# Two PSUM banks shared by three users, V of the first batch loaded by block, and matmuls on zeros between the real ones: a chunked attention with an MLP behind it

## The chip, the cores and the metric

The kernel runs on one core of one Trainium2 chip. A core has a matrix engine (TensorE, PE in the profile; its weight loads are a row of their own, PEld), a vector engine (VectorE, DVE), a scalar engine for activation functions (ScalarE, ACT), a general engine (GpSimd, POOL) and an engine that only issues transfers here (SyncE, SP). Every engine works through its own queue in order; semaphores hold an instruction back until what it needs is there. The metric is the device time of one execution in microseconds, as the median of the runs. Matrix products are written to PSUM, eight banks of 2 KB per partition; everything else lives in SBUF or in HBM.

## What is computed

There are 4 batches of 8 heads, 768 positions and head size 64. Each head's queries are taken in chunks of 32. A chunk sees 8 memory keys, its own 32 positions, 16 positions to the left and 8 to the right. The result goes, head by head side by side, through a two-layer MLP with 512 inputs, 2048 hidden columns and 512 outputs.

```python
for c in range(nc):                       # chunks of 32 positions
    l_start = max(0, c_start - left_ctx)  # 16 to the left
    r_end = min(S, c_end + right_ctx)     # 8 to the right
    k_full = np.concatenate([mem_k, k_ctx], axis=2)
    v_full = np.concatenate([mem_v, v_ctx], axis=2)
    scores = scale * np.matmul(q_c, k_full.transpose(0, 1, 3, 2))
    a = softmax(scores)
    out[:, :, c_start:c_end] = np.matmul(a, v_full)
...
h = x @ w_in
s = np.sin(alpha * h)
g = h + s * s / (alpha + 1e-09)
return g @ w_out
```

All inputs and the output are float32; the kernel multiplies in bfloat16 and accumulates in float32.

## The kernel before

The work is ordered by hand: each engine runs its instructions in the order in which the program writes them, and the framework only adds semaphores and picks slots for tiles. A pool with `bufs=n` has n slots per tag; a new tile waits until a slot's last user is done.

**Blocks.** Attention works on 8 blocks (NJ) of 96 queries (three chunks). For a block, `qk_exp` (L244) multiplies the block's keys (104 columns with the 8 memory keys among them, from `kTi`) with its queries (`qT`) for all 8 heads into a score tile `sc`, and takes the exponential in three activations, one for each chunk, with a mask column of `biasm` as the bias. `pv` (L268) multiplies the result `pt` with the block of V (`vw`, with a column of ones for the sum) into `ot`; VectorE takes the reciprocal of the sums (L278) and scales (L279) into `x_blk`. `xt` (L286) transposes `x_blk` on TensorE into `xtp`, and VectorE copies it into `xT` (L292). `burst` (L294) runs these over the blocks, with a product `lag` steps behind its scores and the transpose one step behind the product.

**Preparing q and k.** They arrive as rows; `pair_up` (L206, VectorE) puts two heads side by side, `t_k` and `t_q` (L221, L236) transpose on TensorE, and ScalarE and VectorE copy the result into `kTi` and `qT`. A k or q pair of one head pair is a "piece"; there are 8 to a batch. `put_memk` (L146, VectorE) writes the memory keys of a batch into `kTi`; `put_memv` (L140) the memory values into `vw`.

**MLP.** `l1` (L311) makes one of 16 blocks (`ft`) of 128 hidden columns for all 768 positions: 8 matmuls into `hT` (two banks), the sine on ScalarE into `u` (L322), its square on ScalarE (L327) or, where `dve_sq` says so, on VectorE (L325), and then `gT = s / alpha + hT` on VectorE (L328). `l2` (L334) is a generator: 6 output tiles `o` of 128 positions, each 16 matmuls over `ft`, copied out by VectorE (L351) or ScalarE (L353) and stored by SyncE (L354). It is not run at once: `Stream.take(n)` draws n matmuls from it at places in later work, so that layer 2 of batch i is spread over the attention and the layer 1 of batch i+1.

**Order.** For each batch i: layer 1 (16 blocks, with 2 layer-2 matmuls drawn per block, 3 in the last batch; for i = 1, 2 the pieces of the next batch are put in at fixed blocks, `at_ft`); for i = 0 the 8 pieces come after the blocks; then `put_memk(i + 1)` (L410), the loads of k and q for batch i+2, `burst(i + 1)`, and the loads of V for batch i+2. The first batch's pieces and its `burst` stand ahead of the loop (L358 to L378).

**PSUM.** `big` has three slots of two banks for `sc`, `ot`, `hT` and two of three transpose tiles of the pieces at the start; `opp` has one bank for `o`; `atp` has one bank for `xtp` and the other transpose tiles (`t_tile`, L215).

**Loads.** k, q, V and the weights are converted to bfloat16 on the way, by DMAs that POOL issues one after the other (`dma_start` on `nc.gpsimd`): k and q of batch 0 as 8 pairs (L101), four DMAs for all of V (`load_v_all`, L122), eight of w_in, k and q of batch 1, four of w_out, V of batch 1. Between them POOL makes the mask `biasm` (L169 to L183, 13 selects).

Of the kernel before, what the change touches and what calls it, by code (L numbers as in the profile page):

```python
# [9 lines left out]
P = 128  # L10
QW = 96
NEG = -30000.0
# [33 lines left out]
def kernel(  # L46
# [30 lines left out]
    big = ctx.enter_context(tc.tile_pool(name="big", bufs=3, space=bass.MemoryType.PSUM))  # L77
    opp = ctx.enter_context(tc.tile_pool(name="opp", bufs=1, space=bass.MemoryType.PSUM))
    atp = ctx.enter_context(tc.tile_pool(name="atp", bufs=1, space=bass.MemoryType.PSUM))

# [32 lines left out]
    def load_qk(b):  # L113
# [6 lines left out]
        return kb, qb  # L120

    def load_v_all(b):  # L122

# [22 lines left out]
    def put_memk(b):  # L146
# [3 lines left out]
        )  # L150


    for vw in vws:
# [8 lines left out]
    for b in range(B):  # L162
        nc.sync.dma_start(memk_f[NM * b:NM * b + NM], mem_k[b].rearrange("h n d -> n h d"))
    nc.sync.dma_start(memv_f[64:72].rearrange("n b h d -> n (b h) d"),
                      mem_v.rearrange("b h n d -> n (b h) d"))
    nc.scalar.copy(memk_bf[:], memk_f[:])
    nc.scalar.copy(memv_st[64:72], memv_f[64:72])
    load_v_all(0)
    nc.gpsimd.memset(biasm[:], NEG)  # L169
    steps = (  # L170
        (0, ((0, 0.0), (56, NEG), (64, 0.0), (72, NEG))),
        (1, ((32, 0.0), (96, NEG))),
        (2, ((64, 0.0),)),
        (3, ((16, 0.0), (56, NEG), (64, 0.0), (72, NEG))),
        (4, ((64, 0.0), (120, NEG))),
    )
    for col, seq in steps:
        for thr, val in seq:
            nc.gpsimd.affine_select(
                out=biasm[:, col:col + 1], in_=biasm[:, col:col + 1],  # L180
                compare_op=ALU.is_gt, fill=val, base=thr,
                pattern=[[0, 1]], channel_multiplier=-1,
            )  # L183
    with nc.allow_non_contiguous_dma(reason="alpha transpose load"):
# [4 lines left out]
    for pt in pts:  # L189
        nc.vector.memset(pt[:, H * QW:H * QW + 32], 0.0)  # L190
    nc.vector.reciprocal(inv_alpha[:], alpha_sb[:])

# [22 lines left out]
    def t_tile():  # L215
        state["t"] += 1
        if state["t"] % state["pools"] == 0:
            return atp.tile([P, 6, P], BF, name="tt_a", tag="at")
        return big.tile([P, 6, P], BF, name="tt_b", tag="big")
# [24 lines left out]
    def qk_exp(j):  # L244
# [10 lines left out]
        for m in range(3):  # L255
            col = m
            if j == 0 and m == 0:
                col = 3
            if j == NJ - 1 and m == 2:
                col = 4  # L260
            nc.scalar.activation(  # L261
                pt[:, 0:H * QW].rearrange("p (g e c) -> p e g c", g=4, e=2)[:, :, :, 32 * m:32 * m + 32],
                sc[:, :, 0:4 * QW].rearrange("p g (e c) -> p g e c", e=4)[:, :, :, 32 * m:32 * m + 32],
                ACTF.Exp, bias=biasm[:, col:col + 1], scale=0.125,
            )
# [20 lines left out]
    def xt(xT, j, x_blk):  # L286
        xtp = atp.tile([P, KT, QW], BF, name="xtp", tag="at")
        for kt in range(KT):
# [5 lines left out]
    def burst(b, stream, shares, lag):  # L294
# [3 lines left out]
        for s in range(NJ + lag + 1):  # L298
            n = shares[s] if s < len(shares) else 0
            if s < NJ:  # L300
                ptl[s] = qk_exp(s)
            stream.take(n // 2)
            if 0 <= s - lag < NJ:
# [30 lines left out]
    def l2(i, gT, last=False):  # L334
        for s in range(NSUB):
            if last and s % 3 == 1:
                o = atp.tile([P, d_model], F32, name="o_a", tag="at")
            elif last and s % 3 == 2:
                o = big.tile([P, d_model], F32, name="o_b", tag="big")
            else:  # L340
                o = opp.tile([P, d_model], F32, name="o", tag="o")
            for ft in range(FT):
# [16 lines left out]
    for n in range(2 * HP):  # L359
        (t_k if n % 2 == 0 else t_q)(prs[n], n // 2)  # L360
        if n + 2 < 2 * HP:
            prs.append(pair_up(kq[n % 2], (n + 2) // 2))
    mt = atp.tile([P, HP, 32], BF, name="mt", tag="at")
    for hp in range(HP):
# [3 lines left out]
    put_memv(0)  # L368
    put_memv(1)
    for c in range(8):  # L370
        load_w_in(c)
# [5 lines left out]
    stream = Stream()  # L377
    xT = burst(0, stream, (), 3)  # L378

    for i in range(B):  # L380
# [6 lines left out]
        state["pools"] = 1  # L387

        def piece(n):
            while len(pieces) < min(n + 3, 2 * HP):  # L390
                pieces.append(pair_up(*srcs[len(pieces)]))
            (t_k if n % 2 == 0 else t_q)(pieces[n], n // 2)

        for ft in range(FT):
            dve_sq = (ft % 2 == 1) if i == 0 else (ft % 4 == 3)
            if 0 < i < B - 1:
                if ft == 0:
                    pieces += [pair_up(*srcs[n]) for n in range(2)]
                if ft in at_ft:
                    piece(at_ft[ft])  # L400
            l1(i, ft, xT, gT, dve_sq)
            if 1 <= ft:
                stream.take(3 if last else 2)
        stream.add(l2(i, gT, last))
        if not last:
            if i == 0:
                state["pools"] = 3
                for n in range(2 * HP):
                    piece(n)
            put_memk(i + 1)  # L410
            if i + 2 < B:
                kq_next = load_qk(i + 2)
            if i == 0:
                xT = burst(i + 1, stream, (4,) * 12, 4)
            else:
                xT = burst(i + 1, stream, (5, 6, 7, 7, 7, 7, 7, 7, 7, 7), 1)
            stream.take(3)
            if i + 2 < B:
# [33 lines left out]
```

## Time and profile before

| what | value |
|---|---|
| runs | 279.32, 276.13, 277.3 us; median 277.3 |
| profiled execution | 276.12 us, span 274.4 us, mean granted clock of TensorE 0.98 |
| TensorE busy | 220.0 us, 80% of the span |
| ScalarE busy | 169.8 us, 62% |
| VectorE busy | 150.6 us, 55% |
| moved by the DMA queues | 21.12 MB, mean 77 GB/s |

In rows of the timeline the first number is the start in us from the beginning of the span, the second the time from the first start to the last end of the merged instructions, then engine, line, operation, output <- inputs, sizes and how many. What stands in brackets is how long the engine was idle before, and what ended that idle time. The row PEclk of the page gives the clock granted to TensorE in tenths, in 40 slices of 6.86 us.

### The profile page before, as it was taken

What the parts mean: (1) busy time and instruction counts of PE and PEld (TensorE: products, weight loads), DVE (VectorE), ACT (ScalarE), POOL (GpSimd) and SP (SyncE); (2) the same over time, 40 slices, a digit from 0 to 9 for tenths busy, and PEclk for the clock granted to TensorE, in tenths of its full rate; (3) what the DMA queues carried; (4) which work ended last, traced back from release to release, by engine and by line L of the source; (5) the groups of instructions that cost most, each with busy time, mean ns of one, the idle gap of its engine ahead of it and who ended that gap; (6) DMA issues with size and microseconds to landing.
All of it is one profiled execution on the core that took longest, in us unless ns stands there. A gap on an engine that the chain in (4) does not pass through costs nothing.

```text
span 274.4 us, 4340 instructions
## 1 busy us (share of the span) xinstructions
PE 220.0 (80%) x1706; PEld 126.6 (46%) x1732; DVE 150.6 (55%) x284; ACT 169.8 (62%) x258; POOL 41.4 (15%) x62
## 2 busy tenths in 40 slices
PE   0463988884799799984998898984999889798994
PEld 0352744442545456552454455652455445454441
DVE  2352828898427867675254667776155365576000
ACT  2666727874996199986536199896546178575000
POOL 8984551000530000170000000000000000000000
PEclk9999999999799999999799999999799999999999
DMA  7999999990399900299921101001011110101222
GB/s 79 181 118 129 197 205 206 183 87 3 45 198 156 93 0 0 52 170 147 88 76 41 38 0 41 0 0 41 38 42 38 41 38 0 38 4 38 76 76 76
DMA packets 53740, 21.12 MB, mean 77 GB/s; under 512 B 36312, under 2 KB 50648, under 8 KB 53720
## 3 DMA queue, kind: packets, MB, share of 16 engines
q0 software_dynamic: 47648, 14.42, 73.9%
q1 hardware_dynamic: 6072, 6.43, 7.5%
q8 instruction: 13, 0.21, 0.3%
q14 instruction: 7, 0.06, 0.1%
HBM read 28.95 MB, written 6.29 MB: 128 GB/s over the span
## 4 chain that ended last, share of the span: by engine, by line
PE 53%; ACT 13%; DVE 11%; DMA 11%; POOL 5%; issue 5%; DVEq 0%; POOLq 0%; ACTq 0%
PE o L343 22%; PE hT L315 18%; DMA w_out_sb<-in_moe_w_out_dram 6%; ACT u L322 5%; DMA w_in_sb<-in_moe_w_in_dram 5%; DVE gT L328 4%; ACT s L327 3%; PE o_a L343 3%; PE o_b L343 2%; DVE s L325 2%; DVE o_sb L351 2%; ACT o_sb L353 2%; PE sc L248 2%; PE ot L274 2%; ACT pt L261 1%
## 5 line engine op out<-in xcount | busy, mean ns | idle before, releaser
L315 PE MATMUL hT<-xT,w_in_sb 128*128 128x384 bf16 x512 | 94.4, 332 | 2.7 <-DVE gT L328 1.7
L343 PE MATMUL o<-w_out_sb,gT 128*128 128x512 bf16 x296 | 84.3, 387 | 12.8 <-DVE o_sb L351 5.8
L328 DVE SCALAR_TENSOR_TENSOR gT<-s,inv_alpha,hT 128x768 bf16<-128x768 f32 x64 | 64.9, 1014 | 40.3 <-ACT s L327 37.5
L322 ACT ACTIVATE u<-hT,alpha_sb 128x768 f32<-128x768 f32 x64 | 57.5, 898 | 43.3 <-PE hT L315 43.3
L315 PEld LDWEIGHTS <-w_in_sb 128*128 128x128 bf16 x512 | 50.1, 99 | 39.4 <-issue 6.7
L343 PEld LDWEIGHTS <-gT 128*128 128x128 bf16 x384 | 34.4, 98 | 43.1 <-issue 13.5
L261 ACT ACTIVATE pt<-sc,biasm 128x256 bf16<-128x256 f32 x96 | 37.7, 484 | 24.6 <-PE sc L248 24.5
L327 ACT ACTIVATE s<-u 128x768 f32<-128x768 f32 x44 | 37.1, 843 | 1.4
L278 DVE RECIPROCAL rinv<-ot 96x8 f32<-96x8 f32 x32 | 6.5, 203 | 30.5 <-PE ot L274 30.0
L279 DVE TENSOR_TENSOR x_blk<-ot,rinv 96x512 bf16<-96x512 f32 x32 | 22.0, 687 | 1.1
L325 DVE TENSOR_TENSOR s<-u 128x768 f32<-128x768 f32 x20 | 19.1, 956 | 3.4 <-ACT u L322 3.3
L248 PE MATMUL sc<-qT,kTi 64*128 64x96 bf16 x256 | 12.4, 229 | 8.6 <-DVE kTi L147 7.9
L274 PE MATMUL ot<-vw,pt 128*128 128x65 bf16 x256 | 15.0, 207 | 4.7 <-DMA vw<-in_v_dram 3.9
L274 PEld LDWEIGHTS <-pt 128*128 128x128 bf16 x256 | 13.3, 107 | 11.2 <-issue 4.7
L224 PEld LDWEIGHTS <-pr 128*128 128x128 bf16 x96 | 7.5, 114 | 19.6 <-DVE pr L208 18.2
L292 DVE COPY xT<-xtp 128x384 bf16<-128x384 bf16 x32 | 11.2, 350 | 7.6 <-PE xtp L289 6.7
L248 PEld LDWEIGHTS <-kTi 64*128 64x128 bf16 x256 | 7.6, 105 | 16.1 <-DVE kTi L147 9.1
L289 PE MATMUL xtp<-ident,x_blk 96*128 96x96 bf16 x128 | 11.9, 222 | 2.7 <-DVE xT L292 2.7
L289 PEld LDWEIGHTS <-x_blk 96*128 96x128 bf16 x128 | 9.7, 105 | 8.4 <-DVE x_blk L279 1.5
L224 PE MATMUL tt_b<-ident,pr 128*128 128x128 bf16 x30 | 3.8, 292 | 11.3 <-DVE pr L208 11.3
L116 POOL DMA_DIRECT2D k_bf<-in_k_dram x3 | 2.7, 900 | 62.7 <-DVE kTi L231 36.0
L351 DVE COPY o_sb<-o 128x512 f32<-128x512 f32 x10 | 6.8, 685 | 6.5 <-PE o L343 6.5
(53 smaller groups left out, 148.7 us busy)
## 6 DMA issues: line engine op xcount, KB each, us to landing
out_dram<-o_sb SPq DMA_DIRECT2D x24, 256.0 KB, 2.0
vw<-in_v_dram POOLq DMA_DIRECT2D x8, 384.0 KB, 14.0
k_bf<-in_k_dram POOLq DMA_DIRECT2D x3, 768.0 KB, 7.5
q_bf<-in_q_dram POOLq DMA_DIRECT2D x3, 768.0 KB, 9.9
w_in_sb<-in_moe_w_in_dram POOLq DMA_DIRECT2D x8, 256.0 KB, 10.7
w_out_sb<-in_moe_w_out_dram POOLq DMA_DIRECT2D x4, 512.0 KB, 18.3
k_bf<-in_k_dram POOLq DMA_DIRECT2D x4, 192.0 KB, 6.0
q_bf<-in_q_dram POOLq DMA_DIRECT2D x4, 192.0 KB, 6.5
```

Source lines behind the costliest of these rows:

```text
L248: nc.tensor.matmul(sc[:, e, QW * hp:QW * hp + QW], kTi[64 * e:64 * e + 64, hp, 104 * j:104 * j + P], qT[64 * e:64 * e + 64, hp, QW * j:QW ...
L261: nc.scalar.activation(pt[:, 0:H * QW].rearrange("p (g e c) -> p e g c", g=4, e=2)[:, :, :, 32 * m:32 * m + 32], sc[:, :, 0:4 * QW].rearra ...
L274: nc.tensor.matmul(otv[:, h // 4, h % 4, :], pt[:, QW * h:QW * h + P], vws[b % 2][:, h, j, 0:D + 1])
L279: nc.vector.tensor_tensor(out=x_blk[:].rearrange("p (g e) d -> p g e d", g=2), in0=otv[0:QW, :, :, 0:D], in1=rv.unsqueeze(3).to_broadcast( ...
L289: nc.tensor.transpose(xtp[:, kt, :], x_blk[:, 2 * kt:2 * kt + 2, :].rearrange("p e d -> p (e d)"), ident[0:QW, 0:QW])
L315: nc.tensor.matmul(hT[:, hf, 0:HALF], w_in_sb[:, kt, P * ft:P * ft + P], xT[:, kt, HALF * hf:HALF * hf + HALF], start=(kt == 0), stop=(kt ...
L322: nc.scalar.activation(u[:], hT[:, :, 0:HALF], ACTF.Sin, scale=alpha_sb[:, ft:ft + 1])
L325: nc.vector.tensor_tensor(out=s2[:], in0=u[:], in1=u[:], op=ALU.mult)
L327: nc.scalar.activation(s2[:], u[:], ACTF.Square)
L328: nc.vector.scalar_tensor_tensor(out=gT[:, ft, :].rearrange("p (e c) -> p e c", e=2), in0=s2[:], scalar=inv_alpha[:, ft:ft + 1], in1=hT[:, ...
L343: nc.tensor.matmul(o[:], gT[:, ft, P * s:P * s + P], w_out_sb[:, ft, :], start=(ft == 0), stop=(ft == FT - 1),)
L351: nc.vector.tensor_copy(o_sb[:], o[:])
```

## The change

1. **PSUM.** The pools `opp` and `atp`, one bank each, become one pool `smp` with two slots of one bank. `o`, `xtp`, `mt` and the transpose tiles that used `atp` all draw from it. In the last batch `o` no longer alternates over three pools.
2. **V of batch 0.** `load_v_all(0)` (4 DMAs) becomes `load_v(0, j)` for each of the 8 blocks: two DMAs each, the rows left of and in the block's first part, and the rest. The mask is made ahead of them, with 8 selects instead of 13 and its columns in another order.
3. **Matmuls on zeros.** `spin(n)` multiplies a tile of zeros, 128x128 by 128x512, n times into a `big` tile that nothing reads: 10 at the start, 2 after each of the first 8 pieces, and 1 at each step of the first `burst`.
4. **Order.** The reciprocal of alpha moves from the start to after `put_memv`. `put_memk(i + 1)` moves from ahead of `burst(i + 1)` to behind `burst(i)`. In batch 0 three pair copies are made in layer 1 (block 12), and after each of the 8 pieces 4 layer-2 matmuls are drawn. `lag` goes from 3 to 2 in the first `burst` and from 4 to 3 in the second, where each of 11 steps draws 3 matmuls instead of 12 steps 4.
5. **Squares of batch 0.** Every third block's square is on VectorE instead of every second's.

```diff
-    opp = ctx.enter_context(tc.tile_pool(name="opp", bufs=1, space=bass.MemoryType.PSUM))
-    atp = ctx.enter_context(tc.tile_pool(name="atp", bufs=1, space=bass.MemoryType.PSUM))
+    smp = ctx.enter_context(tc.tile_pool(name="smp", bufs=2, space=bass.MemoryType.PSUM))
...
+    def load_v(b, j):
+        vw = vws[b % 2]
+        lo = QW * j - 16
+        r0 = max(0, -lo)
+        nc.gpsimd.dma_start(
+            vw[r0:64, :, j, 0:D], v[b, :, lo + r0:lo + 64, :].rearrange("h p d -> p h d")
+        )
+        n = min(56, S - (QW * j + 48))
+        nc.gpsimd.dma_start(
+            vw[72:72 + n, :, j, 0:D],
+            v[b, :, QW * j + 48:QW * j + 48 + n, :].rearrange("h p d -> p h d"),
+        )
...
+    zeros = consts.tile([P, 512], BF, name="zeros")
+    nc.vector.memset(zeros[:], 0.0)
+
+    def spin(n):
+
+        z = big.tile([P, 512], F32, name="z", tag="big")
+        for _ in range(n):
+            nc.tensor.matmul(z[:], zeros[:, 0:P], zeros[:])
+
+    spin(10)
...
-    load_v_all(0)
     nc.gpsimd.memset(biasm[:], NEG)
...
+    for j in range(NJ):
+        load_v(0, j)
...
-    nc.vector.reciprocal(inv_alpha[:], alpha_sb[:])
...
-            return atp.tile([P, 6, P], BF, name="tt_a", tag="at")
+            return smp.tile([P, 6, P], BF, name="tt_a", tag="sm")
...
-        xtp = atp.tile([P, KT, QW], BF, name="xtp", tag="at")
+        xtp = smp.tile([P, KT, QW], BF, name="xtp", tag="sm")
...
             if s < NJ:
                 ptl[s] = qk_exp(s)
+            if b == 0:
+                spin(1)
...
-            if last and s % 3 == 1:
-                o = atp.tile([P, d_model], F32, name="o_a", tag="at")
-            elif last and s % 3 == 2:
-                o = big.tile([P, d_model], F32, name="o_b", tag="big")
-            else:
-                o = opp.tile([P, d_model], F32, name="o", tag="o")
+            o = smp.tile([P, d_model], F32, name="o", tag="sm")
...
         (t_k if n % 2 == 0 else t_q)(prs[n], n // 2)
+        spin(2)
...
     put_memv(1)
+    nc.vector.reciprocal(inv_alpha[:], alpha_sb[:])
...
-    xT = burst(0, stream, (), 3)
+    xT = burst(0, stream, (), 2)
+    put_memk(1)
...
-            dve_sq = (ft % 2 == 1) if i == 0 else (ft % 4 == 3)
+            dve_sq = ft % 3 == 1 if i == 0 else ft % 4 == 3
...
+            if i == 0 and ft == 12:
+                pair_to(3)
...
                     piece(n)
-            put_memk(i + 1)
+                    stream.take(4)
...
-                xT = burst(i + 1, stream, (4,) * 12, 4)
+                xT = burst(i + 1, stream, (3,) * 11, 3)
             else:
                 xT = burst(i + 1, stream, (5, 6, 7, 7, 7, 7, 7, 7, 7, 7), 1)
+            if i + 2 < B:
+                put_memk(i + 2)
```

More of the change, by code (lines that the diff above doesn't have):

```diff
@@ L165 @@
                       mem_v.rearrange("b h n d -> n (b h) d"))
+    nc.gpsimd.memset(biasm[:], NEG)
+    nc.gpsimd.memset(biasm[:, 0:1], 0.0)
+    for c0, c1, thr, val in (
+        (1, 2, 16, 0.0), (0, 2, 56, NEG), (0, 2, 64, 0.0), (0, 2, 72, NEG),
+        (2, 4, 64, 0.0), (3, 4, 120, NEG), (4, 5, 32, 0.0), (4, 5, 96, NEG),
+    ):
+        nc.gpsimd.affine_select(
+            out=biasm[:, c0:c1], in_=biasm[:, c0:c1],
+            compare_op=ALU.is_gt, fill=val, base=thr,
+            pattern=[[0, c1 - c0]], channel_multiplier=-1,
+        )
     nc.scalar.copy(memk_bf[:], memk_f[:])
     nc.scalar.copy(memv_st[64:72], memv_f[64:72])
-    load_v_all(0)
[L169 to L183, printed above, removed]
+    for j in range(NJ):
+        load_v(0, j)
     with nc.allow_non_contiguous_dma(reason="alpha transpose load"):
@@ L255, in qk_exp @@
         for m in range(3):
[L256 to L260, printed above, removed]
+            col = ((1 if j == 0 else 0), 4, (3 if j == NJ - 1 else 2))[m]
             nc.scalar.activation(
@@ L387, with pair_to @@
         state["pools"] = 1
+        def pair_to(n):
+            while len(pieces) < min(n, 2 * HP):
+                pieces.append(pair_up(*srcs[len(pieces)]))
         def piece(n):
-            while len(pieces) < min(n + 3, 2 * HP):
-                pieces.append(pair_up(*srcs[len(pieces)]))
+            pair_to(n + 3)
             (t_k if n % 2 == 0 else t_q)(pieces[n], n // 2)
+        if 0 < i < B - 1:
+            pair_to(2)
         for ft in range(FT):
-            dve_sq = (ft % 2 == 1) if i == 0 else (ft % 4 == 3)
[L396 to L400, printed above, removed]
+            dve_sq = ft % 3 == 1 if i == 0 else ft % 4 == 3
+            if 0 < i < B - 1 and ft in at_ft:
+                piece(at_ft[ft])
+            if i == 0 and ft == 12:
+                pair_to(3)
             l1(i, ft, xT, gT, dve_sq)
```

2 lines of the change are left out of this document (1 added, 1 removed).

## The prediction

> **What bounds the kernel now.** I read the page's slices and clock first, then the chain of waits, then the timeline stage by stage, then who waited for whom.
>
> ```profile
> span 274.4 us, 4340 instructions
> PEclk9999999999799999999799999999799999999999
> 31.28 16.66 DMA w_out_sb<-in_moe_w_out_dram
> ```
>
> The clock granted to TensorE (PE) dips three times, each time where an MLP stage hands over to the next attention. The last line, from the chain, misleads: it puts 16.66 us on a load of w_out, which layer 1 doesn't read. So I leave the chain for the timeline. The start:
>
> ```profile
> 8.74 0.25 DVE L191 RECIPROCAL inv_alpha<-alpha_sb 128x16 f32<-128x16 f32 x1 [5.93 <-DMA alpha_sb<-in_moe_alpha_dram]
> 9.36 0.82 PE L224 MATMUL tt_b<-ident,pr 128*128 128x128 bf16 x6 [9.36 <-DVE pr L208]
> 18.83 1.14 PE L248 MATMUL sc<-qT,kTi 64*128 64x96 bf16 x24 [0.71 <-DVE kTi L147]
> 25.14 0.60 PE L274 MATMUL ot<-vw,pt 128*128 128x65 bf16 x8 [3.95 <-DMA vw<-in_v_dram]
> 28.17 1.20 ACT L261 ACTIVATE pt<-sc,biasm 128x256 bf16<-128x256 f32 x3 [0.76 <-PE sc L248]
> 34.12 0.64 PE L274 MATMUL ot<-vw,pt 128*128 128x65 bf16 x8
> 36.33 8.01 PE L315 MATMUL hT<-xT,w_in_sb 128*128 128x384 bf16 x32
> 41.09 0.15 PEld L315 LDWEIGHTS <-w_in_sb 128*128 128x128 bf16 x1 [0.17 <-issue]
> 54.29 2.76 PE L315 MATMUL hT<-xT,w_in_sb 128*128 128x384 bf16 x16 [0.34 <-DVE gT L328]
> 67.29 0.51 PE L224 MATMUL tt_a<-ident,pr 128*128 128x128 bf16 x6 [3.88 <-DVE pr L208]
> ```
>
> Read there: the first pair copy waits behind the alpha load; the first scores begin at 18.8; the first V product waits 3.95 us for V; layer 1 begins at 36.3. The clock column says full speed here, but the spacing says half: a weight load at 41.1 us comes 0.17 + 0.15 = 0.32 us after the one before, against 2.76/16 = 0.17 us per matmul later, and six transposes take 0.82 us at 9.4 but 0.51 at 67.3. The first attention and about 5 us of layer 1 (36.3 to 41.4) run cold. Then the MLP of batch 0 and the hand-overs:
>
> ```profile
> 40.34 0.84 ACT L327 ACTIVATE s<-u 128x768 f32<-128x768 f32 x1
> 48.01 0.88 ACT L322 ACTIVATE u<-hT,alpha_sb 128x768 f32<-128x768 f32 x1
> 54.37 0.88 ACT L322 ACTIVATE u<-hT,alpha_sb 128x768 f32<-128x768 f32 x1
> 60.65 2.76 PE L315 MATMUL hT<-xT,w_in_sb 128*128 128x384 bf16 x16 [0.34 <-DVE gT L328]
> 65.95 1.01 DVE L328 SCALAR_TENSOR_TENSOR gT<-s,inv_alpha,hT 128x768 bf16<-128x768 f32 x1
> 73.72 0.40 PE L248 MATMUL sc<-qT,kTi 64*128 64x96 bf16 x8 [0.70 <-DVE kTi L147]
> 126.08 1.28 ACT L261 ACT_TABLE_LOAD   x1
> 129.03 0.34 PE L248 MATMUL sc<-qT,kTi 64*128 64x96 bf16 x8 [3.69 <-DVE kTi L147]
> 132.89 0.65 PE L274 MATMUL ot<-vw,pt 128*128 128x65 bf16 x8
> 189.63 1.28 ACT L261 ACT_TABLE_LOAD   x1
> 191.92 0.50 PE L248 MATMUL sc<-qT,kTi 64*128 64x96 bf16 x8 [2.81 <-DVE kTi L147]
> 193.18 0.15 PEld L343 LDWEIGHTS <-gT 128*128 128x128 bf16 x1 [0.28 <-issue]
> 195.69 0.41 PE L274 MATMUL ot<-vw,pt 128*128 128x65 bf16 x8
> ```
>
> Four layer-1 blocks take 54.37 - 48.01 = 6.36 us, 1.59 each. At both later hand-overs the scores wait 3.69 and 2.81 us for the copy at L147, put_memk, which stands in VectorE's (DVE's) queue behind the last gT; then the clock is down (layer 2's weight loads come 0.28 + 0.15 = 0.43 us apart at 193). Last, the stages as wholes, and layer 2's own waits:
>
> ```profile
> 73.70:93.70 20.00, 17.38 (x207) 9.84 (x212) 10.65 (x27) 12.48 (x28) 4.16 (x4) 1.00 1.86 157
> 93.70:128.00 34.30, 30.24 (x202) 17.77 (x204) 24.07 (x37) 30.46 (x38) 5.99 (x6) 1.00 0.56 72
> 217.00:252.00 35.00, 32.40 (x179) 17.50 (x179) 19.59 (x21) 24.94 (x30) 0.00 (x0) 1.00 0.06 24
> PE o L343 <- DVE o_sb L351: 5.8, 7, 1.8
> PE o L343 <- ACT o_sb L353: 4.7, 8, 1.2
> 253.26 3.62 PE L343 MATMUL o_a<-w_out_sb,gT 128*128 128x512 bf16 x16
> 256.72 3.62 PE L343 MATMUL o_b<-w_out_sb,gT 128*128 128x512 bf16 x15
> ```
>
> Columns of the first three: stretch, length, then busy PE, PEld, DVE, ACT, POOL. Attention of batch 1 and layer 1 of batch 3 are bound by TensorE. Layer 1 of batch 1 is bound by TensorE and ScalarE (ACT) alike (30.24 and 30.46). Layer 2 waits 5.8 + 4.7 = 10.5 us for its one output bank. A layer-2 matmul costs (256.72 - 253.26)/16 = 0.216 us warm.
>
> **The change part by part.** The sum is made against the profiled execution, 276.1 us with 274.4 of span; the median of the runs is 277.3, 1.2 above.
>
> *Start to first scores.* The reciprocal leaves the head of DVE's queue. The pair copies then wait for their loads alone:
>
> ```profile
> 7.03 0.75 POOL L103 DMA_DIRECT2D q_bf<-in_q_dram  x1
> DMA to landing us min/median/max: 4.0/6.4/7.4
> 12.40 3.00 POOL L179 TENSOR_SCALAR_AFFINE_SELECT biasm<-biasm 128x1 f32<-128x1 f32 x13
> L194 POOL DMA_DIRECT2D w_in_sb<-in_moe_w_in_dram x8: 740/760/1631, 15.4 to 25.8; - x8
> 18.70 1.63 POOL L194 DMA_DIRECT2D w_in_sb<-in_moe_w_in_dram  x1 [0.24 <-DMA vw<-in_v_dram]
> vw<-in_v_dram POOLq DMA_DIRECT2D x8, 384.0 KB, 14.0
> GB/s 79 181 118 129 197 205 206 183 87 3 45 198 156 93 0 0 52 170 147 88 76 41 38 0 41 0 0 41 38 42 38 41 38 0 38 4 38 76 76 76
> ```
>
> The second line is for the pair loads. The last of them is issued at 7.0 and lands by 14.4; its copy could be in the transposes by about 15 and the scores follow by 16.5, so at best some 2.3 us are gained. Against that stand 16 zero matmuls between the transposes: 0.43 us each cold (the 0.43 spacing of a 128x512 matmul above), 0.216 warm, so 3.5 to 6.9 us of TensorE where 18.83 - 9.36 less 8 x 0.82 us of transposes leaves 2.9, and warm 8 x 0.51 leaves 5.4. The first ten run before data is there and are free. I take -1.2; ends -2.3 and +2.
>
> *V by block.* Sixteen DMAs of 512 and 448 rows stand for four. At 0.76 us of issue each (the w_in row, 512 rows too) they hold POOL 12 us from about 9.7 (7.8, and 8 selects of the mask row's 13) to 22. The first block lands in time for the first scores, and the 3.95 us wait goes. What is late next is ScalarE's exponentials: 0.3 + 8 x 1.20 + a tail of 2.4 (34.12 to 36.33 today, and the hand-over to the product) = 12.3, plus an estimated 1.4 for slots, since the zero tile takes one of the three big PSUM slots at each step: 13.7 against 36.33 - 18.83 = 17.5. -3.8; ends -5.2 and +3.5 (cold, today's (34.12 - 25.14)/7 = 1.28 per step plus the zero matmul's 0.43 and a wait for its slot, 2 us in all). Queued behind the V issues are w_in, k, q and w_out. w_in then starts some 6.5 us later, at 22, and is needed at about 31, so I cost this at nothing; the lane rival below is its price if that cover goes.
>
> *Clock into layer 1.* If the zero matmuls keep TensorE from idling, the first 16 layer-1 matmuls cost 0.17 and not 0.32 us: 16 x 0.15 = -2.4.
>
> The Trainium skill ("TensorE: Matmul & The Clock Gate", Part 1) says the clock opens after about 3.4 us of sustained activity; the trace shows 5.1 (36.3 to 41.4). The same page's Part 4 says that transposes don't count as activity. By that rule this term and the first one would be lost, which is the first rival.
>
> *Squares: a third on DVE instead of half.* The rate isn't set by either engine's sum but by three PSUM slots: matmul 1.38, sine 0.88, square 0.84, gT 1.01 and the hand-overs and queueing, some 4.7 us per slot, /3 = 1.58. The new split leaves that chain as it is, and the third pair copy in block 12 lies beside it: 0; ends -0.8 and +0.4.
>
> *Hand-over of batch 0.* Eight pieces (transposes) now each draw four layer-2 matmuls, 32 x 0.216 = 6.9 us, into a stretch where TensorE mostly waits. With the pair copies done early the stretch from the last layer-1 matmul (60.65 + 2.76 = 63.4, 27.1 after the start of layer 1) to the scores at 73.7 goes from 10.3 to about 8 x 0.51 + 6.9 = 11.1. Layer 1's matmuls end at about +25 instead of +27.1. Start of layer 1 to scores: 37.4 -> 36.2, -1.2, the clock term included.
>
> *Where those 32 go missing.* Attention of batch 1 takes 33 + 3 instead of 48 + 3: 15 x 0.216 = 3.2 in a TensorE-bound stage, and one step of lag: -3.6 (ends -1 and -5). Layer 1 of batches 1 and 2 takes 28 and 26 instead of 30 and 30: nothing, ScalarE binds there as well. Layer 1 of batch 3 has 26 left instead of 37: 11 x 0.216 = -2.4 (from 0, if ScalarE's floor takes over at once).
>
> *put_memk earlier.* The scores of batches 2 and 3 can follow the last layer-1 matmul. Late next is the exponential behind the last sine and the table load (126.08 + 1.28 = 127.4); its product at about 127.4 + 1.2 + 0.1 = 128.7 instead of 132.9: -4.2, and by the same count 189.63 + 1.28 + 1.3 = 192.2 instead of 195.7, -3.5. The copy now stands ahead of the next pair copies, +0.25 twice. Together -7.2; ends -3 and -8.
>
> *Two shared banks.* The next output tile can start while the last one is copied out; transposes take the other bank, so it may meet those instead. Of the 10.5 us I take about half, -5.5 (ends 0 and -9).
>
> The same page of the Trainium skill (Part 1, the thin-M case) reports that PSUM double-buffering gave no further gain there. By that this term would be 0 and the time 5.5 longer; the waits of up to 1.8 us for o_sb speak against it here.
>
> Sum: -1.2 - 3.8 - 1.2 - 3.6 - 2.4 - 7.2 - 5.5 = -24.9, so 251.2 in a profiled execution, and **252.5** as a median.
>
> **Rivals.** *The clock isn't held.* The zero matmuls then cost 0.43 each on the path: start +1.2, attention +3.5, hand-over +0.8 with its longer transposes, and the other terms (-18.7) stand: 262.9, as a median 264. For it: half clock throughout the first attention today. Against: cold, the steps fill TensorE entirely, and the 32 matmuls from 36.3 on did open it.
>
> *The shared banks meet.* A piece's tile is held until ScalarE and then DVE have copied it, and a new output tile waits for that instead: the 5.5 are lost: 258. For it: in-order TensorE, two banks for three users. Against: pieces come only every second block.
>
> *Slower: the lanes.* A POOL DMA waits for the one eight before it (the fifth w_in for the first V load, above). V, w_in, and k, q with w_out make successive rounds, so w_in lands at about 9.7 + 3L for a landing time L, and layer 1 starts there if that is after 31. The scores of batch 1 come at 9.7 + 3L + 36.2 against 73.7; the later terms give back 18.7. So it turns slower from L = 15.5; at L = 18 it is 276.1 + 26.2 - 18.7 = 283.6. The 14.0 us of the V row is near that, but those loads were six times as large and stood behind k and q; eight of the small ones are some 0.5 MB as written, at the page's 118 GB/s or more about 4 us.
>
> **How the numbers follow.** Forecast 0.62; clock not held 0.14; banks meet 0.18; lanes 0.04; a sum of small losses that ends within a per cent 0.02. The range: the forecast's own unknowns, start and first attention, allow 246 to 259; the two milder rivals reach 264; beyond lie the lanes and a few per cent on each side. 246 to 264. About 1% is what a measurement can tell from no change: faster 0.94, same 0.02, slower 0.04.
>
> **What would show it.** In the changed profile: first scores near 17.6 and the first V product with no wait on V; layer 1 from about 31 with weight loads 0.17 us apart; no dip of the clock at the three hand-overs; no wait of sc on L147; waits of o on o_sb well under 10.5 us. Scores later than 19, or layer 1 later than 36, would break the first half; 50 and more with waits on w_in would be the lanes. Waits on L147 that turn into waits on ScalarE would break the second.

## The result, and the profile after

The changed kernel takes **249.74 us** (median; 248.82 to 250.45) against 278.31 us for the kernel before on the same chip (276.13 to 279.32): a ratio of 0.898, with a 95% interval of 0.891 to 0.905. It is 10% faster. The forecast was 252.5 in a range of 246 to 264. The profiled execution has a span of 247.7 us, where 274.4 stood. One execution of e3 below (the profiled one) and one of e5 took over 1.5% longer than the fastest of their run, at a lower granted clock; the medians in brackets leave it out.

The page of the changed kernel, its span, the clock row and the loads of w_in (the last number is the median from issue to landing):

```profile
span 247.7 us, 4445 instructions
PEclk9799999999999999999999999999999999999999
w_in_sb<-in_moe_w_in_dram POOLq DMA_DIRECT2D x8, 256.0 KB, 7.8
```

The three dips at the hand-overs are gone; a new one stands in the second slice: from 8.51 to 11.92 us the granted clock is 0.50. The lines have moved: put_memk is L159 now (L147 before), the scores L267, layer 1 L332, layer 2 L355. The start and the first hand-over in the timeline of the changed kernel:

```profile
6.23 0.51 PE L243 MATMUL tt_b<-ident,pr 128*128 128x128 bf16 x6 [0.76 <-DVE pr L227]
10.41 0.82 PE L243 MATMUL tt_a<-ident,pr 128*128 128x128 bf16 x6 [0.66 <-DVE pr L227]
11.88 0.52 PE L258 MATMUL tt_b<-ident,pr 128*128 128x128 bf16 x6
12.67 0.51 PE L243 MATMUL tt_b<-ident,pr 128*128 128x128 bf16 x6
17.51 0.34 PE L267 MATMUL sc<-qT,kTi 64*128 64x96 bf16 x8 [0.81 <-DVE kTi L159]
19.64 0.40 PE L289 MATMUL ot<-vw,pt 128*128 128x65 bf16 x8
22.97 5.99 POOL L213 DMA_DIRECT2D w_in_sb<-in_moe_w_in_dram  x8
30.54 0.33 PE L332 MATMUL hT<-xT,w_in_sb 128*128 128x384 bf16 x1
31.15 3.90 PE L332 MATMUL hT<-xT,w_in_sb 128*128 128x384 bf16 x23 [0.28 <-DVE xT L307]
51.72 3.81 PE L332 MATMUL hT<-xT,w_in_sb 128*128 128x384 bf16 x21
55.37 0.50 PE L243 MATMUL tt_a<-ident,pr 128*128 128x128 bf16 x6
55.70 1.03 PE L355 MATMUL o<-w_out_sb,gT 128*128 128x512 bf16 x4
65.18 0.34 PE L267 MATMUL sc<-qT,kTi 64*128 64x96 bf16 x8
113.21 0.34 PE L267 MATMUL sc<-qT,kTi 64*128 64x96 bf16 x8
114.66 1.28 ACT L276 ACT_TABLE_LOAD   x1
117.21 0.42 PE L289 MATMUL ot<-vw,pt 128*128 128x65 bf16 x8 [1.44 <-ACT pt L276]
173.83 0.42 PE L289 MATMUL ot<-vw,pt 128*128 128x65 bf16 x8 [1.16 <-ACT pt L276]
```

The scores start at 17.51 instead of 18.83, no product waits for V, and layer 1 starts at 30.54 instead of 36.33, at full speed: 23 matmuls in 3.90 us are 0.17 each. At the later hand-overs the scores no longer wait on put_memk; what is late is the exponential behind its table load, with 1.44 and 1.16 us of waiting. Stretches as wholes (attention of batch 1; layer 1 of batch 1 up to the first product of batch 2; layer 1 of batch 3) and the waits around the shared banks, of the changed kernel:

```profile
65.16:81.52 16.36, 15.00 (x197) 8.51 (x197) 9.74 (x26) 12.89 (x29) 2.93 (x4) 1.00 2.05 187
81.52:117.20 35.68, 32.70 (x229) 18.69 (x227) 25.00 (x39) 31.62 (x42) 6.01 (x6) 1.00 0.85 74
194.50:226.30 31.80, 30.26 (x171) 16.42 (x168) 20.36 (x21) 24.29 (x30) 0.00 (x0) 1.00 0.06 21
```

```profile
PE o L355 <- ACT o_sb L365: 1.7, 5, 0.5
PE tt_a L258 <- DVE o_sb L363: 1.5, 1, 1.5
PE o L355 <- DVE o_sb L363: 1.5, 2, 0.7
PE o L355 <- ACT qT L259: 0.6, 1, 0.6
PE sc L267 <- DVE kTi L159: 0.8, 1, 0.8
```

The waits for the output banks fall from 10.5 us to 1.7 + 1.5 = 3.2, and 1.5 + 0.6 appear in which a piece's tile and an output tile meet. Where the 26.7 us between the two spans went, stage by stage:

| stage (profiled execution) | before | after | difference |
|---|---|---|---|
| start to first scores | 18.83 | 17.51 | -1.3 |
| first scores to first layer-1 matmul | 17.50 | 13.03 | -4.5 |
| layer 1 of batch 0 to scores of batch 1 | 37.39 | 34.64 | -2.75 |
| attention of batch 1 | 20.01 | 16.36 | -3.65 |
| layer 1 of batch 1 to first product of batch 2 | 39.16 | 35.67 | -3.5 |
| rest of attention 2 | 22.54 | 20.75 | -1.8 |
| layer 1 of batch 2 to first product of batch 3 | 40.26 | 35.87 | -4.4 |
| rest of attention 3 | 21.39 | 20.75 | -0.6 |
| layer 1 of batch 3 until layer 2 waits for no gT | 35.96 | 31.76 | -4.2 |
| layer 2 to the end | 21.36 | 21.36 | 0 |

### The profile page after: what moved, and what is told of

Read it like the earlier page. It is cut to its first block, busy times and chain, and to the rows that moved or that the text cites. A ratio compares the mean times of both kernels' runs of the same rounds, so it can differ in the third digit from the quotient of the medians.

```text
span 247.7 us, 4445 instructions
## 1 busy us (share of the span) xinstructions
PE 221.4 (89%) x1769; PEld 122.5 (49%) x1769; DVE 147.0 (59%) x282; ACT 172.3 (70%) x261; POOL 48.1 (19%) x70
## 4 chain that ended last, share of the span: by engine, by line
PE 55%; ACT 25%; DVE 11%; issue 5%; DMA 2%; SPq 1%; DVEq 0%; ACTq 0%
PE o L355 27%; PE hT L332 18%; ACT u L339 8%; ACT s L344 6%; ACT pt L276 5%; DVE gT L345 3%; PE ot L289 3%; DVE x_blk L294 2%; DMA memv_f<-in_mem_v_dram 2%; PE sc L267 2%; ACT o_sb L365 2%; ACT L276 2%; DVE s L342 2%; PE xtp L304 1%; ACT kTi L244 1%
## 5 line engine op out<-in xcount | busy, mean ns | idle before, releaser
L355 PE MATMUL o<-w_out_sb,gT 128*128 128x512 bf16 x384 | 100.2, 379 | 4.2 <-ACT o_sb L365 1.7
L332 PE MATMUL hT<-xT,w_in_sb 128*128 128x384 bf16 x512 | 91.7, 326 | 4.0 <-DVE gT L345 3.6
L332 PEld LDWEIGHTS <-w_in_sb 128*128 128x128 bf16 x512 | 49.3, 98 | 39.2 <-issue 6.2
L355 PEld LDWEIGHTS <-gT 128*128 128x128 bf16 x384 | 33.9, 97 | 33.3 <-issue 3.9
L276 ACT ACTIVATE pt<-sc,biasm 128x256 bf16<-128x256 f32 x96 | 37.4, 490 | 13.7 <-PE sc L267 13.5
L344 ACT ACTIVATE s<-u 128x768 f32<-128x768 f32 x47 | 39.6, 843 | 1.5
L365 ACT COPY o_sb<-o 128x512 f32<-128x512 f32 x12 | 7.0, 582 | 30.2 <-PE o L355 30.1
L342 DVE TENSOR_TENSOR s<-u 128x768 f32<-128x768 f32 x17 | 16.2, 955 | 2.7 <-ACT u L339 2.6
L289 PEld LDWEIGHTS <-pt 128*128 128x128 bf16 x256 | 11.8, 97 | 10.9 <-ACT pt L276 3.6
L363 DVE COPY o_sb<-o 128x512 f32<-128x512 f32 x12 | 8.2, 687 | 14.4 <-PE o L355 14.3
L171 PE MATMUL z<-zeros 128*128 128x512 bf16 x37 | 14.1, 468 | 2.2 <-DVE zeros L165 1.3
L289 PE MATMUL ot<-vw,pt 128*128 128x65 bf16 x256 | 13.0, 193 | 3.4 <-ACT pt L276 3.0
L267 PE MATMUL sc<-qT,kTi 64*128 64x96 bf16 x256 | 11.0, 205 | 1.8 <-DVE kTi L159 0.8
```

The costliest lines, as they stand in the source:

```text
L171: nc.tensor.matmul(z[:], zeros[:, 0:P], zeros[:])
L267: nc.tensor.matmul(sc[:, e, QW * hp:QW * hp + QW], kTi[64 * e:64 * e + 64, hp, 104 * j:104 * j + P], qT[64 * e:64 * e + 64, hp, QW * j:QW ...
L276: nc.scalar.activation(pt[:, 0:H * QW].rearrange("p (g e c) -> p e g c", g=4, e=2)[:, :, :, 32 * m:32 * m + 32], sc[:, :, 0:4 * QW].rearra ...
L289: nc.tensor.matmul(otv[:, h // 4, h % 4, :], pt[:, QW * h:QW * h + P], vws[b % 2][:, h, j, 0:D + 1])
L332: nc.tensor.matmul(hT[:, hf, 0:HALF], w_in_sb[:, kt, P * ft:P * ft + P], xT[:, kt, HALF * hf:HALF * hf + HALF], start=(kt == 0), stop=(kt ...
L342: nc.vector.tensor_tensor(out=s2[:], in0=u[:], in1=u[:], op=ALU.mult)
```

## The experiments

Each run takes the changed kernel and undoes or alters one thing. Every profile is split at the first layer-1 matmul: the time up to it scatters from profile to profile even with the same code ahead of it, while the time from there to the end hardly does. In the table a ratio is to the kernel before; "rest" is the span less the first layer-1 matmul. The kernel before has 274.4 - 36.33 = 238.1 there.

| run | what differs from the changed kernel | median us | ratio, 95% interval | first scores | layer 1 | rest |
|---|---|---|---|---|---|---|
| after | nothing | 249.74 | 0.898, 0.891 to 0.905 | 17.51 | 30.54 | 217.2 |
| c1 | nothing, run again | 249.88 | 0.905, 0.899 to 0.910 | 19.07 | 32.10 | 217.1 |
| e1 | no matmuls on zeros | 251.55 | 0.906, 0.897 to 0.914 | 18.10 | 31.33 | 218.3 |
| e2 | V of batch 0 whole | 255.68 | 0.921, 0.913 to 0.928 | 17.69 | 35.79 | 217.1 |
| e3 | put_memk ahead of its burst again | 258.72 (257.94) | 0.929, 0.919 to 0.939 | 17.00 | 32.97 | 226.6 |
| e4 | own PSUM bank for `o` again | 258.48 | 0.931, 0.923 to 0.940 | 18.37 | 32.93 | 224.8 |
| e5 | no layer-2 draws in the hand-over | 250.41 (250.02) | 0.907, 0.901 to 0.913 | 18.70 | 31.73 | 216.5 |
| e6 | reciprocal of alpha first again | 251.53 | 0.912, 0.909 to 0.915 | 19.57 | 32.60 | 217.1 |
| e7 | every second square on VectorE again | 251.11 | 0.909, 0.904 to 0.914 | 17.46 | 30.48 | 218.1 |
| e8 | zeros at the start and the pieces only | 251.78 | 0.913, 0.910 to 0.916 | 18.33 | 31.61 | 218.3 |
| e9 | zeros in the first attention only | 253.30 | 0.918, 0.913 to 0.923 | 17.56 | 34.82 | 217.2 |
| n1 | layer 2 started inside layer 1 | 261.20 | 0.947, 0.941 to 0.952 | 17.37 | 30.39 | 229.5 |
| n2 | the same, and six more zeros | 261.25 | 0.947, 0.941 to 0.953 | 17.09 | 30.12 | 230.2 |

### Two banks or one each

```diff
-    smp = ctx.enter_context(tc.tile_pool(name="smp", bufs=2, space=bass.MemoryType.PSUM))
+    opp = ctx.enter_context(tc.tile_pool(name="opp", bufs=1, space=bass.MemoryType.PSUM))
+    smp = ctx.enter_context(tc.tile_pool(name="smp", bufs=1, space=bass.MemoryType.PSUM))
...
-            o = smp.tile([P, d_model], F32, name="o", tag="sm")
+            if last and s % 3 == 1:
+                o = smp.tile([P, d_model], F32, name="o_a", tag="sm")
...
+                o = opp.tile([P, d_model], F32, name="o", tag="o")
```

> The changed kernel with one bank for the layer-2 output and one for the transposes, and the old rotation over three banks in the last batch. Theory (sharing two banks takes half of the 10.5 us of waits away): waits of o on its copy back to 8 us or more, plus 3 to 5.5 us: 253 to 255. Rival (the waits only change place, or lie beside other work): within 1 us of 249.7.

The rest takes 224.8 us instead of 217.2: +7.6, and the median is 8.7 us higher, more than the 3 to 5.5 expected. Its table of waits (us in total, times, longest):

```profile
PE o L361 <- DVE o_sb L369: 9.1, 9, 2.0
PE o L361 <- ACT o_sb L371: 2.5, 7, 0.5
```

So 11.6 us of waiting come back where the shared banks left 3.2, and of these 8.4 us nine tenths reach the end. The loss is spread: +0.6, +0.4, +1.7, +2.8 and +2.1 us over the hand-over, attention 1, the batches 1 and 2 from layer 1 to layer 1, and the last batch. The first attention, ahead of the rest, is longer too, 14.56 us instead of 13.03: the transposes there wait 1.2 us in all for copies of xT, and the granted clock is 0.50 from 22.19 to 25.60 us. How much of that is the bank's isn't separated. The rival "the banks meet" falls: what meets is small (1.5 + 0.6 us above). The Trainium skill ("TensorE: Matmul & The Clock Gate", Part 1) reports no further gain from PSUM double-buffering for a thin-M kernel; here the second bank is worth 7.6 us in the span. In this kernel the matmul that waits for its bank stands in TensorE's queue ahead of attention or layer-1 work that could run.

### put_memk

```diff
-    put_memk(1)
...
+            put_memk(i + 1)
             if i == 0:
...
-            if i + 2 < B:
-                put_memk(i + 2)
```

> The changed kernel with put_memk where it was, ahead of the next attention. Theory (the copy behind the last gT holds the scores at each hand-over, and lets the clock fall): waits of sc on the copy of 3 to 4 us at both later hand-overs, the clock dips there again, plus 5 to 8 us: 255 to 258. Rival (ScalarE with its last sine and the table load binds just as late): plus 1 to 2 us: 251 to 252.

The median in brackets is 8.2 us higher, within what the theory expected. The timeline shows the cause at the two later hand-overs, where the kernel before waited 3.69 and 2.81 us:

```profile
119.23 0.50 PE L267 MATMUL sc<-qT,kTi 64*128 64x96 bf16 x8 [3.66 <-DVE kTi L159]
180.75 0.50 PE L267 MATMUL sc<-qT,kTi 64*128 64x96 bf16 x8 [3.92 <-DVE kTi L159]
```

At the first hand-over no such wait comes back: the scores at 67.70 us follow without one, where the kernel before had 0.70. The two batches from layer 1 to layer 1 take 61.1 and 61.5 us instead of 56.4 and 56.6: the profile has +9.6 there, more than the medians have in all. What comes back is more than the two waits, 7.6. Around each of them the granted clock is 0.50 for 6.83 us (118.19 to 125.01 and 179.62 to 186.45), while after the change it stays at 1.00 there; how much of the remaining 2.0 us belongs to that isn't separated.

### V by block

```diff
-    for j in range(NJ):
-        load_v(0, j)
+    load_v_all(0)
```

> The changed kernel with V of batch 0 loaded whole, in four transfers behind the new mask. Theory (the wait for V bounds the first attention): the first V product waits until about 26 us for a transfer of V, TensorE idles 5 us and more and its clock falls, layer 1 starts near 36 instead of 30.5: 255 to 258. Rival (the exponentials bound it, V is hidden): 249 to 250.5, and the first layer-1 matmul within 1 us of 30.5.

From nearly the same first scores (17.69 and 17.51), layer 1 starts 5.25 us later (35.79 against 30.54), 5.07 of it in the first attention, and the rest is the same, 217.1. From its timeline:

```profile
24.69 0.60 PE L288 MATMUL ot<-vw,pt 128*128 128x65 bf16 x8 [4.92 <-DMA vw<-in_v_dram]
27.17 0.50 PE L266 MATMUL sc<-qT,kTi 64*128 64x96 bf16 x8
28.59 0.34 PE L266 MATMUL sc<-qT,kTi 64*128 64x96 bf16 x8
```

The wait of 4.92 us is the one that the kernel before had with 3.95. The clock is down after it (eight matmuls of the scores take 0.50) and up again by 28.6 (0.34). The median is 5.9 us higher. So four large loads are worse than sixteen small ones here, although POOL spends 10.15 to 22.97 us on issuing these. The lane rival needed landing times of 15.5 us; w_in lands in 7.8, and layer 1 waits for xT, not for it.

### The matmuls on zeros

All out:

```diff
-    spin(10)
...
-            if b == 0:
-                spin(1)
...
-        spin(2)
```

> The changed kernel without any matmul on zeros. Theory (they hold the clock): the first attention and the first 16 matmuls of layer 1 run at half clock again, weight loads 0.32 us apart; layer 1 starts about 0.5 to 1.5 us later than the 30.5 us of the changed kernel and loses 2.4 us at its head, so 252.5 to 254. Rival (the zeros only take time and a PSUM slot): 248.5 to 249.7, with the first matmuls of layer 1 already 0.17 us apart.

Only those at each step of the first `burst` out:

```diff
-            if b == 0:
-                spin(1)
```

> The changed kernel with the zeros before and between the first transposes, and none in the first attention. If the attention's own matmuls keep the clock open once it is open: weight loads of layer 1 0.17 us apart from the first one, 249 to 250, no worse than the changed kernel. If the zeros of the attention are what holds it: half clock at the start of layer 1, 251.5 to 253.

Only those at the start and behind the pieces out:

```diff
-    spin(10)
...
-        spin(2)
```

> The changed kernel with the zeros in the first attention alone. If these hold the clock: half clock until about 22 us, full clock at layer 1, the scores within 0.5 us of 17.5: 249.5 to 251. If the zeros at the start are what opens it and those in the attention only keep it: the attention begins cold, runs at 1.7 us a step or more, and layer 1 starts 2 us late or more: 251.5 to 254.

Without any zeros the first attention is cold until about 28.1 us and yet takes 13.23 us, hardly more than the 13.03 with them. From there the granted clock is 1.00, but only to 31.5 us; then it is 0.50 for 3.41 us, and the price shows in layer 1 alone. The weight loads of e1 there:

```profile
32.21 0.15 PEld L329 LDWEIGHTS <-w_in_sb 128*128 128x128 bf16 x1 [0.17 <-issue]
...
34.45 0.15 PEld L329 LDWEIGHTS <-w_in_sb 128*128 128x128 bf16 x1 [0.17 <-issue]
34.77 2.30 PEld L329 LDWEIGHTS <-w_in_sb 128*128 128x128 bf16 x14 [0.17 <-issue]
```

Nine loads stand 0.32 us apart, then 14 lie within 2.30. The rest is 218.3 in e1 and in e8, against 217.2: **1.1 us** is what a warm first layer 1 is worth. In e9 it is 217.2 again, so the zeros in the attention are what warms layer 1. But there they begin with a cold clock and cost more than they give. From its timeline:

```profile
17.56 0.50 PE L266 MATMUL sc<-qT,kTi 64*128 64x96 bf16 x8 [0.70 <-DVE kTi L159]
23.65 0.50 PE L266 MATMUL sc<-qT,kTi 64*128 64x96 bf16 x8
24.08 0.61 PE L171 MATMUL z<-zeros 128*128 128x512 bf16 x1
25.60 0.50 PE L266 MATMUL sc<-qT,kTi 64*128 64x96 bf16 x8
31.99 0.53 PE L288 MATMUL ot<-vw,pt 128*128 128x65 bf16 x8
32.53 0.38 PE L171 MATMUL z<-zeros 128*128 128x512 bf16 x1
34.82 0.33 PE L331 MATMUL hT<-xT,w_in_sb 128*128 128x384 bf16 x1
```

A cold step takes 25.60 - 23.65 = 1.95 us, and the attention 34.82 - 17.56 = 17.26 instead of 13.03. So the zeros at the start, which bring nothing by themselves (e8 is no faster than e1), keep the later ones from costing 4 us. All together they are worth 251.55 - 249.74 = 1.8 us in the medians; the intervals of the two ratios overlap. The median of e1 lies between its theory and its rival; e8 and e9 came out as the second of their two cases has it.

The zeros don't always hold the clock. Nine profiles have them in both places and V by block; in seven of these the first attention takes 13.02 or 13.03 us. In e4 the clock fell in it for 3.41 us, as above. In e3, whose code up to layer 1 is that of the changed kernel except for a copy behind the attention, it fell at 19.20 us and came back at 29.44, and the attention took 32.97 - 17.00 = 15.97 us. This stretch of e3 (length, busy PE, granted clock, DMA):

```profile
19.20:29.44 10.24, 9.50 (x110) 0.50 1.21 108
```

### Draws in the hand-over

```diff
                     piece(n)
-                    stream.take(4)
...
-                xT = burst(i + 1, stream, (3,) * 11, 3)
+                xT = burst(i + 1, stream, (4,) * 12, 4)
```

> The changed kernel without the 4 layer-2 matmuls after each piece of the first hand-over; the second attention draws 12 times 4 with a lag of 4, as before. Theory (32 matmuls fill idle TensorE time there and are missing later, where TensorE binds): the hand-over gets shorter by 2 to 4 us, the second attention longer by 3 to 3.6, layer 1 of the last batch by 2.4 or a little more: 252 to 254. Rival (they only move, what they fill they also lengthen): within 1 us of 249.7.

The rival was right. The stage to the scores of batch 1 falls by 2.7 us (31.92 instead of 34.64), their attention grows by 3.7 (20.06 instead of 16.36), and all the rest together is 1.7 us shorter (164.5 instead of 166.2): 216.5 against 217.2, and 250.41 (250.02) against 249.74 in the medians. From its timeline:

```profile
52.42 4.30 PE L332 MATMUL hT<-xT,w_in_sb 128*128 128x384 bf16 x24 [0.50 <-DVE gT L345]
60.26 0.51 PE L258 MATMUL tt_a<-ident,pr 128*128 128x128 bf16 x6 [1.60 <-DVE pr L227]
63.65 0.30 PE L267 MATMUL sc<-qT,kTi 64*128 64x96 bf16 x6
```

Without the draws the scores follow the last layer-1 matmul by 63.65 - 56.72 = 6.9 us, not by the 10.3 of the kernel before. The hole that was to be filled had shrunk without them.

### Squares

```diff
-            dve_sq = ft % 3 == 1 if i == 0 else ft % 4 == 3
+            dve_sq = ft % 2 == 1 if i == 0 else ft % 4 == 3
```

> The changed kernel with every second square of batch 0 on VectorE, as before. Theory (three PSUM slots set the rate of layer 1, not the split): sines 1.55 to 1.60 us apart in batch 0, within 0.6 us of the changed kernel. Rival (VectorE's sum binds): 1.5 us or more slower.

The rest takes 218.1 instead of 217.1 to 217.2, and the median is 1.2 us above that of the changed kernel run beside it, between the 0.6 of the theory and the 1.5 of the rival. First and last sine of batch 0's layer 1 in the timeline of e7:

```profile
32.43 0.90 ACT L339 ACTIVATE u<-hT,alpha_sb 128x768 f32<-128x768 f32 x1 [3.59 <-PE hT L332]
56.15 0.90 ACT L339 ACTIVATE u<-hT,alpha_sb 128x768 f32<-128x768 f32 x1
```

and in that of the changed kernel run again:

```profile
34.05 0.90 ACT L339 ACTIVATE u<-hT,alpha_sb 128x768 f32<-128x768 f32 x1 [3.58 <-PE hT L332]
57.27 0.89 ACT L339 ACTIVATE u<-hT,alpha_sb 128x768 f32<-128x768 f32 x1
```

Fifteen steps take 23.72 us with half of the squares on VectorE and 23.22 with a third: 1.58 and 1.55 each, so the spacing is what the theory said. The whole stage to the scores of batch 1 differs by 35.67 - 34.64 = 1.0 us; half of that lies behind the last sine.

### The reciprocal, and the changed kernel again

```diff
+    nc.vector.reciprocal(inv_alpha[:], alpha_sb[:])
...
-    nc.vector.reciprocal(inv_alpha[:], alpha_sb[:])
```

> The changed kernel with the reciprocal of alpha back at the head of VectorE's queue. Theory: the first pair copy starts at 8.7 to 8.9 instead of 5.8 us, the scores 0.8 to 1.3 us later than 17.5: 250.5 to 251. Rival (the q pair, which landed at 7.85, or the later pairs set the pace): under 0.4 us, 249.5 to 250.1.

> The changed kernel as it is, once more, beside the three below: 248.5 to 251. What is looked for is the start: in the eight runs so far the first layer-1 matmul came between 30.5 and 35.8 us, while from there to the end the runs that share the rest of the program took 217.1 or 217.2 us each. If that holds, this one shows 217.1 again, whatever its start.

With the reciprocal first, the first transposes begin at 9.46 us and the scores at 19.57. That looks like 2 us lost, but the unchanged kernel, run again, starts its scores at 19.07. Its transposes:

```profile
6.80 0.51 PE L243 MATMUL tt_b<-ident,pr 128*128 128x128 bf16 x6 [1.34 <-DVE pr L227]
8.59 0.82 PE L258 MATMUL tt_b<-ident,pr 128*128 128x128 bf16 x6 [0.85 <-DVE pr L227]
12.33 0.85 PE L258 MATMUL tt_b<-ident,pr 128*128 128x128 bf16 x6
13.82 0.85 PE L243 MATMUL tt_b<-ident,pr 128*128 128x128 bf16 x6
15.32 0.51 PE L258 MATMUL tt_a<-ident,pr 128*128 128x128 bf16 x6
```

The clock opens under the ten zeros at the start, is down again at 8.59, and up again only for the sixth piece, at 15.32; in the first profile it was up by 11.88. A cold piece with its two zeros takes 13.82 - 12.33 = 1.5 us, a warm one 12.67 - 11.88 = 0.8 in the first profile. Two more cold pieces account for 1.4 of the 1.56 us between the two starts. The profiles with this code ahead of the scores put them between 17.0 and 19.1, so they don't settle what the reciprocal's place is worth. The times do better: all four executions of e6 (251.37 to 251.67 us) lie above all ten of the changed kernel (248.61 to 251.01; not all on the same chip), and the medians differ by 1.8 us, more than either expectation. In its profile TensorE idles 3.75 us behind the first ten zeros, and the transposes are cold up to 13.84 us.

### Starting layer 2 earlier

An attempt to go further. Output tiles 0 and 1 of batch 0 are opened while its layer 1 still runs, and their matmuls drawn as the blocks of gT appear; likewise in the last batch from block 10 on.

```diff
-        for s in range(NSUB):
-            o = smp.tile([P, d_model], F32, name="o", tag="sm")
+        if i == 0:
+            head = [(0, range(13)), (1, range(12)), (0, range(13, 16)), (1, range(12, 16))]
...
+        if i == 0:
+            stream.add(l2(i, gT, last))
...
+            if i == 0:
+                stream.take(1 if ft >= 3 else 0)
```

> The changed kernel with layer 2 of batches 0 and 3 begun inside their own layer 1: 13 matmuls of batch 0 (one per block, three blocks behind), 9 of batch 3; two output tiles are open at a time, the transposes of the first hand-over all use the big slots, and the second attention draws 20 instead of 33. Theory (slots bind layer 1 of batch 0, so that TensorE idles there about 4 us, and in the last blocks of batch 3 about 2): the second attention is 2 to 2.8 us shorter, the end 1.5 to 2 us, layer 1 of batch 0 no longer: 245 to 246.5. Rival (the draws only move, as in the run without draws): 249 to 250.5.

The second run adds two zeros at the start and four behind the first piece.

> The kernel with early layer 2, with 12 zero matmuls at the start instead of 10 and 6 after the first transposes instead of 2, so that TensorE doesn't idle while the first q pair is on its way. Theory (the clock opens by chance of its window and closes in that gap): the first six transposes of the second piece take 0.51 us, the scores come by 17.5 and layer 1 by 31, 0 to 1.5 us below the kernel with early layer 2. Rival (cold, the added zeros delay the second piece): 0.5 to 2 us above it.

Both missed by the same thing. From the timeline of n1:

```profile
48.58 0.58 PE L365 MATMUL o<-w_out_sb,gT 128*128 128x512 bf16 x1 [11.91 <-DMA w_out_sb<-in_moe_w_out_dram]
48.97 2.76 PE L332 MATMUL hT<-xT,w_in_sb 128*128 128x384 bf16 x8
```

The first early matmul needs w_out, which lands only at 48.5 us; layer 1 stands behind it in the queue for 11.91 us and goes on cold (8 matmuls in 2.76 us, 1.46 later). Where w_out was there it did what was meant: from the first layer-1 matmul of batch 3 to the end n1 takes 51.36 us and n2 51.39, the changed kernel 53.12. In that stretch it is some 1.7 us faster; this part wasn't run by itself. The six zeros show nothing that the scatter of the start doesn't.

## Why the prediction was right, and where it wasn't

It was right in its time: 251.2 for the profiled execution, where 247.7 of span and the 1.7 us around it (276.1 less 274.4 before) make 249.4; as medians it is 252.5 against 249.74. Undoing the parts one by one costs 5.9 (V), 8.2 (put_memk), 8.7 (banks), 1.8 (zeros), 1.8 (reciprocal), 1.2 (squares) and 0.3 us (draws) in the medians, 27.9 of the 28.6 that the change brings. The runs stand on several chips, on which the kernel before had medians of 276.24 to 278.31, so the sum is good to a microsecond or two. Three of the four largest terms were the three large causes. That the total came so close is in part luck: the two terms for the draws, 6.0 us together, are nearly nothing when the draws are undone, and the clock term was twice too large, while V, put_memk and the banks brought more than their terms and the squares more than nothing.

Two sums of the prediction are off by 0.1: 25 + 11.1 is 36.1, and 251.2 + 1.2 is 252.4.

- **Start to scores** (-1.2): -1.3 in the profile, but the same code scatters by 2 us. The agreement proves little; the reciprocal alone is worth about 1.8 in the medians.
- **First attention** (-3.8): -4.5, and 5.07 when undone. The working holds: no wait for V, and the 24 exponentials, which begin at 17.95, end at 27.60 us, 1.2 for each block. The estimated 1.4 us for slots was too much by 0.7 (13.03 instead of 13.7).
- **Clock into layer 1** (-2.4): the mechanism holds, the size was off. Nine or ten matmuls were cold without the zeros, not 16, some 1.4 us, of which 1.1 reach the end; that the sine, square and slots behind them hide the rest is argued. They were cold because the clock fell again at the end of the attention (31.5 us in e1), not because it hadn't opened.
- **Squares** (0, ends -0.8 and +0.4): 1.0 us, just beyond the end. The step that failed is "the new split leaves that chain as it is". A square on VectorE stands in the queue with gT, which frees the slots; that this is the way is argued, the 0.03 us per block is measured.
- **Hand-over and "where those 32 go missing"** (36.2 and -3.6): 34.64 and -3.65 stand in the table, but as causes they cancel. The step that failed is that the 10.3 us were a stretch "where TensorE mostly waits": e5 shows it down to 6.9 without the draws, and with them it is 9.7, not 11.1. In layer 1 of batch 3 the draws are worth 33.19 - 31.76 = 1.4 us of the 2.4, and the stages between take it back; why these are shorter without the draws stays open.
- **put_memk** (-7.2, ends -3 and -8): 8.2 when undone, just beyond the end. The next thing late was named rightly, the exponential behind its table load: its product comes 1.27 us after the load's end at 115.94, where the sum has 1.3. The two waits alone make 7.6; the sum had no term for the clock, which is at half around them, and whether that is the rest is argued.
- **Two shared banks** (-5.5 of 10.5): 7.6 in the span behind the first layer-1 matmul. "About half" was the choice that failed: of the waits that come back nine tenths reach the end.
- **Rivals.** "The clock isn't held" happened in part: in the two profiles of the changed kernel the clock fell only among the first transposes, but in that of e3 for 10.24 us of the first attention, with the same code. Its step was priced rightly, 1.95 us in e9 against 2, and the whole too high: 17.5 + 3.5 = 21.0 us for the first attention, where e9 took 17.26 and e3 15.97. "The shared banks meet" and the lanes didn't happen.

## What to carry to other kernels

A wait in an in-order queue costs nearly its whole length when other ready work stands behind it: look for the instruction at the head, and give it a second buffer (8.7 us) or move what it waits for ahead of the longer item on its own queue (8.2 us). Filling a hole with other work pays only if the hole is still there after the other edits; measure it with them in. Keeping the clock up paid only where TensorE set the pace, in the layer-1 matmuls that follow: 1.1 us here. The same filler, started cold, cost 4, and in one profile the clock fell in spite of it and the attention took 2.9 us longer.

## What the runs showed of the hardware

- The same code ahead of the scores let them start between 17.0 and 19.1 us, with the clock reopening at about 11.9 in one profile and 15.3 in another. In the ten profiles with the zeros and the reciprocal at the start as changed (n2 with six more zeros), the granted clock, once up, stays up until the scores (which then start at 17.00 to 17.69), or is at 0.50 for 3.41 us of that time (17.51 and 18.33) or for 6.83 us (18.37 to 19.07). The Trainium skill ("TensorE: Matmul & The Clock Gate", Part 1) describes the activity window as free-running, about 3.4 us long, so that the moment of opening varies between runs. The traces agree: after the first opening every stretch at 0.50 that ends within a span lasts 3.41, 6.83, 10.24 or 13.65 us, one to four times 3.41.
- By that page's rule, a window of sustained activity opens the clock. In e2 it opened within 28.59 - 24.69 = 3.9 us; in e9, with the same instructions nearly end to end from 23.65 us on, it opened only at about 32, more than 8 us later; and in e3 it stayed at half for 10.24 us with TensorE busy for 9.50 of them. The runs don't tell why.
- The row PEclk of the page doesn't show a cold start. For e9 it reads 9 in every slice, though its first attention ran at half speed until about 32 us; the duration of six transposes (0.51 or 0.82 us) or of eight score matmuls (0.34 or 0.50) tells it. A fall after the first opening it does show: 7 in the second slice of the changed kernel, and 5 and 7 in the two slices of e3 from 19.5 to 32.5 us.
